# Reordering the first block pair and the last value tile of a two-branch mixing kernel

## The chip, the cores and the metric

One core of one Trainium2 chip runs the kernel. The metric is the device time of one execution in microseconds (us); lower is better. The profile shows one more execution, taken by the hardware profiler, with five engines: PE (matrix multiply; PEld is its weight load), DVE (vector), ACT (scalar and activation), POOL (GpSimd), and SP, which here issues DMAs.

## What is computed

A linear-attention branch and an expert-lookup branch on the same input `x` (2048 rows of 512) are mixed by a sigmoid gate. All data is float32. Cut to what matters:

```python
# attention: 32 heads of 16
q, k, v = split(x @ wqkv)
pq, pk = q @ w_phi[h], k @ w_phi[h]
phi_q = concat(softmax(pq), softmax(-pq)); phi_k = concat(softmax(pk), softmax(-pk))
kv = einsum("sf,sd->fd", phi_k, v);  z = sum_s phi_k
a  = ((phi_q @ kv) / (phi_q @ z + 1e-6)) @ wo
# experts: 32 heads, 16 x 16 experts, best one of each half
s1, s2 = (x @ w_q)[..., :128] @ k1.T, (x @ w_q)[..., 128:] @ k2.T
e = argmax(s1) * 16 + argmax(s2)
b = sum_h gelu(x . u[e_h]) * v[e_h]
out = g * a + (1 - g) * b,   g = sigmoid(sum(x * gate_w))
```

## The kernel before

The 2048 rows are 16 tiles of 128. float32 products are made of three matmuls of a high part and a low part: the high part is a cast (`x_high`, on ACT for tiles 3 and up), the low part the rest, by a subtraction (`x_low`, on DVE).

Every instruction stands in the program by hand: each engine works through its own queue in the order in which the lines issue, and an instruction that waits holds up all that is behind it on its engine. SP's queue of DMA issues is one of these.

**The key stage** sums phi_k and v over all 16 tiles into one PSUM bank, `kvacc`. Tiles 0 to 4 are handled one by one in the loop `for t in range(5)` (lines 416 to 448). For a tile: `vproj` and `kproj` (twelve matmuls each) make v and pk; `k_diffs` (four DVE operations) writes the softmax exponents; `k_exp` (ACT, line 266) takes the exponential; `k_sum` (DVE, lines 270 and 271) the sums and their reciprocals; `k_mult` (POOL, line 275) scales; `kvacc(t)` (PE, line 282) adds the tile to the bank. Tiles 0 to 2 have their v before the loop. In between, `score` turns two 1 MB slices of w_q at a time into score weights: four matmuls per slice (`score_w`, line 298), a copy into 16-bit planes (`wpl`, line 303), a transposing DMA (`wtp<-wpl`, line 305) and, later, `join_all`: a copy `wtj` (line 314), a cast into `sh` (line 320) and a subtraction on POOL into `sl` (line 321). A slice's buffer is free for the next load when its matmuls are done, so the loads of w_q follow `score_w`.

**The block pairs** (`for t in range(5, NT - 1, 2)`, lines 465 to 539) do tiles 5 and 6, 7 and 8, and so on, with seven products of six matmuls instead of eight (a Strassen-like scheme). `Sums.add` (POOL, lines 175 to 178) forms sums of two x tiles in place; `Sums.high` (ACT, line 183) and `Sums.low` (POOL, line 188) split them; the weights are summed once. The four weight sums are t1 (lines 388, 390 and 442), t2 (389, 441 and 446), `eh`/`el`, and the fourth, t4: a POOL subtraction `t4r` (line 448), a cast `t4h` into a free part of `sh` (line 487, ACT) and a POOL subtraction `t4l` (line 496). Only the last product of a pair uses t4:

```python
a = pks[t] = mm_bank(f"pk{t}")            # first half of pk(t)
prod(a, tile_of(t, 0), b11, True)
act.copy(b, a)                            # "pu" copy, line 483
prod(e, sums(0, 2), b1, True)
prod(b, sums(1, 0), b2, False)
act.copy(c, b)                            # "pv" copy, line 502
prod(a, tile_of(t, 2), b21, False)        # pk(t) complete
...                                       # score, kvacc
prod(b, sums(0, 0), b3, False)
act.copy(d, b)                            # "pk" copy, line 522
prod(c, sums(1, 2), b22, False)
prod(o2, tile_of(n, 2), b4, False)        # the t4 product
```

**The query loop** (lines 910 to 985) has 15 steps. In step a, queries of tile a are made (`front_q`) and their softmax run (`soft_in`, `soft_exp`, line 638, `soft_w`, `soft_b`), scores of tile a+1 are made (`front_s`), tile a-1 is transposed and joined (`planes`, `join`, line 721) and tile a-2 is multiplied by the sums (`mid_num`, line 730, with casts at line 734) and by wo (`back`, lines 839 and 846). Step 1 also ends the key stage: `vproj(15)` runs on PE, its copy `v15()` (ACT, line 254) follows, then `kvacc(15)`, then `kv_final` (ACT, line 869) copies the bank into `kvb`, which step 2's `mid_num(0)` reads. The weights of wo are cast (`wbh`, lines 942 and 978) and subtracted (`wbl`, lines 964 and 982) in the same step.

Of the kernel before, what the change touches and what calls it, by code (L numbers as in the profile page):

```python
# [16 lines left out]
ALU = mybir.AluOpType  # L17
# [18 lines left out]
def mix_kernel(ctx, tc, xT, wqT, wkT, wv, wphi, wo, wq, kk, ug, ev, cst, out):  # L36
    nc = tc.nc
    pe, dve, act, pool, sp = nc.tensor, nc.vector, nc.scalar, nc.gpsimd, nc.sync
# [112 lines left out]
    def x_high(t, ks=slice(0, NK)):  # L151
        (dve.tensor_copy if t < 3 else act.copy)(x_of(t)[0][:, ks], rawx[t][:, ks])  # L152
# [10 lines left out]
    t1r, t2r = t12[:, 0:2], t12[:, 2:4]  # L163
# [101 lines left out]
    def k_exp(t):  # L265
        act.activation(phis[t], phis[t], AF.Exp)  # L266

    def k_sum(t):
        d, st = phis[t], stk[t]
        dve.tensor_reduce(st[:, 64:128], g64(d), axis=AX.X, op=ALU.add)  # L270
        dve.reciprocal(st[:, 128:192], st[:, 64:128])
# [5 lines left out]
    def kvacc(t):  # L277
        n = F + 1 if t < NT - 1 else F
        for g in range(8):
            for c in range(4):  # L280
                h = 4 * g + c
                pe.matmul(acc[32 * c:32 * c + 32, g, :n], phis[t][:, 32 * h:32 * h + 32],
                          vs[t][:, h, :n], start=(t == 0 and g == 0),
                          stop=(t == NT - 1), skip_group_check=True)
# [131 lines left out]
    for t in range(5):  # L416
        if t in (1, 2):
            x_load(t + 6)
        if t > 2:
            vproj(t)()  # L420
        kproj(t)
        k_diffs(t)
        if t in (2, 4):
            join_all()
        score((2, 0, 1, 1, 2)[t])
        if t % 2 == 0:
            for u in (t - 3, t - 2):
                if u >= 0:
                    kvacc(u)
        if t < 3:  # L430
            x_split(t + 3)
        if t == 2:
            x_split(6)
            Sums.add(5)
        if t == 3:
            Sums.high(5)
            Sums.low(5)
        k_exp(t)
        k_sum(t)
        if t == 0:  # L440
            act.copy(t2h, t2r)
            pool.tensor_tensor(t1l, t1r, t1h, op=ALU.subtract)
        if t < 4:
            k_mult(t)
        if t == 0:
            pool.tensor_tensor(t2l, t2r, t2h, op=ALU.subtract)
        if t == 3:
            pool.tensor_tensor(t4r, t4r, t2r, op=ALU.subtract)
    x_high(7)
    x_high(8)  # L450

    def prod(o, left, right, first):
        for i, ((ah, al), (bh, bl)) in enumerate(zip(left, right)):
# [11 lines left out]
    for t in range(5, NT - 1, 2):  # L465
        n = t + 1
        more = [u for u in (t + 4, t + 5) if u < NT]
        for u in more:
            x_load(u)
        if t == NT - 5:  # L470
            rawu = [spare(ug[:, 0:2], "rawu0", [P, 2, NU])]
        elif t == NT - 3:
            rawu.append(spare(ug[:, 2:4], "rawu1", [P, 2, NU]))
            rawe = [spare(ev[:, 0], "rawe0", [P, D])]
        for u in (t + 2, t + 3):
            if u < NT - 1:
                x_low(u)
        if behind:
            k_diffs(behind)
        a = pks[t] = mm_bank(f"pk{t}")  # L480
        prod(a, tile_of(t, 0), b11, True)
        b = mm_bank(f"pu{t}")
        act.copy(b, a)
        if t + 3 < NT:
            Sums.add(t + 2)
        if t == 5:
            act.copy(t4h, by4(t4r))
        if t < NT - 3:
            join_all()
        else:  # L490
            (j6, tp), = joins
            joins.clear()
            tj6 = wa_.tile([P, D], F32, tag="wtj", bufs=1, name="wtj6")
            join_tp(j6, tp, tj6)
        if t == 5:
            pool.tensor_tensor(t4l, by4(t4r), t4h, op=ALU.subtract)
            k_mult(4)
        e = tr_bank(f"pe{t}")
        prod(e, sums(0, 2), b1, True)
        prod(b, sums(1, 0), b2, False)  # L500
        c = mm_bank(f"pv{t}")
        act.copy(c, b)
        prod(a, tile_of(t, 2), b21, False)
        k_diffs(t)
        if behind:
            k_exp(behind)
            k_sum(behind)
            k_mult(behind)
        score(1)
        if t == NT - 3:  # L510
            rawq = stage(wqT, "rawq")
        score(1)
        for u in (t - 3, t - 2):
            if u > 2:
                kvacc(u)
        k_exp(t)
        k_sum(t)
        vn, vt = v_tile(n), v_tile(t)
        act.copy(vn, by16(e))  # L519
        prod(b, sums(0, 0), b3, False)  # L520
        d = pks[n] = mm_bank(f"pk{n}")
        act.copy(d, b)
        prod(c, sums(1, 2), b22, False)
        if t == NT - 3:
            x_split(NT - 1)
        dve.tensor_tensor(vt, by16(c), vn, op=ALU.add)
        dve.tensor_tensor(vn, by16(b), vn, op=ALU.add)
        o2 = d.rearrange("p (c n) -> p c n", c=2)
        prod(o2, tile_of(n, 2), b4, False)
        if t + 3 < NT:  # L530
            Sums.high(t + 2)
            Sums.low(t + 2)
        if t == 7:
            for i in range(2):
                x_parts(i, 11)
        for u in more if n < NT - 4 else ():
            x_high(u)
        k_mult(t)
        behind = n
# [68 lines left out]
    def gelu_act(t):  # L608
        x2, gs = st8[t]["x2"], st8[t]["g"]
        act.activation(gs[:, 3:4], gs[:, 2:3], AF.Copy, scale=-0.5, bias=0.5)  # L610
        act.activation(x2, x2, AF.Tanh)
        act.activation(x2, x2, AF.Identity, bias=gs[:, 3:4], scale=gs[:, 3:4])

    def gelu_out(t):
        px, x2 = st8[t]["G"], st8[t]["x2"]
        pool.tensor_tensor(px, x2, px, op=ALU.mult)
# [18 lines left out]
    def soft_exp(t):  # L635
        d = st8[t]["ph"]
        for i in range(2):
            act.activation(hs(d, i), hs(d, i), AF.Exp)  # L638
# [77 lines left out]
    def join(t):  # L716
        e = st8[t]
        pt = w4.tile([P, 8, P], F32, tag="pt", bufs=1, name=f"pt{t}")
        p16 = pt.rearrange("p g n -> p (g n)").bitcast(U16).rearrange("p (g n j) -> p j g n", j=2, n=P)
        for i in range(2):  # L720
            act.copy(p16[:, :, 4 * i:4 * i + 4, :], e["tp"][i].rearrange("p (j g) n -> p j g n", j=2))  # L721
        e["pt"] = pt
# [187 lines left out]
    for a in range(NT - 1):  # L910
        n, b, z = a + 1, a - 1, a - 2
        owed = min(18, 3 * max(0, a - DEFER))
        left = min(18, 3 * max(0, a - DEFER + 1))
        B, Z = b >= 0, z >= 0
        if Z:
            mid_num(z)
        if B:
            planes(b, 0)
            if Z:
                c_join(z)  # L920
            planes(b, 1)
            front_q(a)
        if owed:
            back(z - 1, owed)
            store(z - 1)
        if a == 1:
            v15 = vproj(NT - 1)
        gelu_in(a)
        if Z:
            num_lo(z)  # L930
        if B:
            soft_in(a, dealt(a, b, z))
            drain(b)
        else:
            for _ in gate(a):
                pass
        gelu_act(a)
        soft_exp(a)
        if a == 1:
            v15()  # L940
            for k in range(2):
                act.copy(wbh[:, k, :], rawo[k])
        if Z and not left:
            back(z)
            store(z)
        if not left:
            mid_mask(a)
        front_s(n, 0)
        if left:
            mid_mask(a)  # L950
            if left < 18:
                back(z, 18 - left)
        if a == 1:
            kvacc(NT - 1)
            cl_.close()
            w4 = ctx.enter_context(tc_pool("w4", "right"))
        front_s(n, 1)
        front_p(n, False)
        soft_w(a)
        soft_sum(a, 0)  # L960
        soft_sum(a, 1)
        if a == 1:
            for k in range(2):
                pool.tensor_tensor(wbl[:, k, :], rawo[k], wbh[:, k, :], op=ALU.subtract)
            wo_load((2, 3))
        best(n, 0)
        soft_y(a, 0)
        soft_y(a, 1)
        soft_p(a)
        if B:  # L970
            join(b)
            gelu_out(b)
            coef(b)
            c_planes(b)
        if a == 1:
            kv_final()
            for k in range(2, NK):
                act.copy(wbh[:, k, :], rawo[k])
        soft_b(a)
        if a == 1:  # L980
            for k in range(2, NK):
                pool.tensor_tensor(wbl[:, k, :], rawo[k], wbh[:, k, :], op=ALU.subtract)
        best(n, 1)
        turn_eq(n)
        gelu_pre(n)
# [124 lines left out]
```

## Time and profile before

| | |
|---|---|
| median of 3 runs | 382.86 us (382.3 to 383.41) |
| the profiled execution | 383.04 us, of which its span is 381.3 us |
| granted TensorE clock | 1.00 |
| PE busy | 367.1 us (96% of the span) |
| DVE busy | 330.0 us (87%) |
| ACT busy | 253.0 us (66%) |
| POOL busy | 204.0 us (53%) |
| DMA | 46.67 MB, mean 122 GB/s |

Times in the rows are us from the start of the span. A timeline row gives start, duration, engine, line, operation, output<-inputs, shape and count; in brackets stands the engine's idle time before it and what ended that.

### The profile page before, as it was taken

How to read it: one execution, taken by the hardware profiler on the slowest of the kernel's cores; microseconds unless marked ns; L12 is line 12 of the kernel's file. 1: busy time of each engine (PE TensorE's matmuls, PEld its weight loads, DVE VectorE, ACT ScalarE, POOL GpSimd, SP SyncE). 2: the span in 40 equal slices, each digit the busy share in tenths (PEclk: the TensorE clock that was granted, in tenths of full speed). 3: DMA queues.
4: the chain of work that ended last, by engine and by line, in shares of the span. 5: the costliest groups of instructions: out<-in, count | busy, mean ns of one | idle time of the engine just before them, and what ended most of it. 6: DMA issues, size and time to landing. Idle time of an engine off the chain costs nothing.

```text
span 381.3 us, 8988 instructions
## 1 busy us (share of the span) xinstructions
PE 367.1 (96%) x3519; PEld 287.5 (75%) x3519; DVE 330.0 (87%) x782; ACT 253.0 (66%) x449; POOL 204.0 (53%) x206
## 2 busy tenths in 40 slices
PE   7997979999999999799999999999999999999996
PEld 3765656677778888578888888888888888888775
DVE  4679888899968858979999999999999999999993
ACT  4584677757666344678677686695686686686741
POOL 1175889898938733756335344364364364364700
PEclk9999999999999999999999999999999999999999
DMA  7865697599664034141541452434513523613211
GB/s 265 314 247 162 224 301 250 180 189 286 236 181 71 4 84 81 58 98 42 110 98 44 83 99 65 89 82 44 126 43 84 124 44 83 126 43 83 60 39 55
DMA packets 72218, 46.67 MB, mean 122 GB/s; under 512 B 63600, under 2 KB 64496, under 8 KB 69872
## 3 DMA queue, kind: packets, MB, share of 16 engines
q1 hardware_dynamic: 71312, 45.24, 44.7%
q10 hardware_dynamic: 864, 0.87, 0.8%
q8 instruction: 27, 0.44, 0.5%
q14 instruction: 15, 0.12, 0.1%
HBM read 26.43 MB, written 4.19 MB: 80 GB/s over the span
## 4 chain that ended last, share of the span: by engine, by line
PE 76%; POOL 7%; DVE 5%; ACT 4%; DMA 4%; issue 3%; ACTq 0%; POOLq 0%
PE po L839 11%; PE s L56 7%; PE s L57 7%; PE s L58 7%; PE po L846 5%; PE pq L56 5%; PE pq L58 4%; PE pq L57 4%; PE pk L455 3%; PE oT L730 3%; DMA wtp<-wpl 2%; PE pp L57 2%; PE pp L58 2%; PE pp L56 2%; PE pu L455 2%
## 5 line engine op out<-in xcount | busy, mean ns | idle before, releaser
L644 POOL TENSOR_TENSOR w<-d,zb 128x512 f32<-128x512 f32 x32 | 40.9, 1296 | 83.4 <-ACT d L638 83.4
L56 PE MATMUL s<-sh,xh 128*128 128x512 f32 x128 | 51.0, 399 | 0.0
L57 PE MATMUL s<-sl,xh 128*128 128x512 f32 x128 | 49.9, 390 | 0.0
L58 PE MATMUL s<-sh,xl 128*128 128x512 f32 x128 | 49.9, 390 | 0.0
L638 ACT ACTIVATE d<-d 128x512 f32<-128x512 f32 x32 | 20.1, 632 | 39.9 <-DVE d L119 31.1
L679 POOL TENSOR_TENSOR d<-d,st 128x512 f32<-128x512 f32 x30 | 31.2, 1062 | 28.4 <-DVE st L673 25.5
L275 POOL TENSOR_TENSOR d<-d,st 128x1024 f32<-128x1024 f32 x16 | 32.5, 2030 | 17.7 <-ACT v L519 7.8
L721 ACT COPY pt<-tp 128x1024 uint16<-128x1024 uint16 x28 | 36.4, 1370 | 0.0
L711 ACT COPY pl<-d 128x1024 uint16<-128x1024 uint16 x28 | 29.2, 1045 | 4.3 <-POOL d L679 4.3
L58 PEld LDWEIGHTS s<-sh,xl 128*128 128x128 f32 x128 | 24.0, 188 | 5.1
L56 PEld LDWEIGHTS s<-sh,xh 128*128 128x128 f32 x128 | 24.0, 188 | 4.7
L57 PEld LDWEIGHTS s<-sl,xh 128*128 128x128 f32 x128 | 24.1, 188 | 4.5
L56 PE MATMUL pq<-wah,xh 128*128 128x512 f32 x64 | 26.8, 418 | 0.0
L648 DVE TENSOR_REDUCE st<-d 128x32 f32<-128x512 f32 x32 | 21.7, 682 | 5.4 <-ACT d L638 3.8
L58 PE MATMUL pq<-wah,xl 128*128 128x512 f32 x64 | 25.1, 392 | 0.0
L57 PE MATMUL pq<-wal,xh 128*128 128x512 f32 x64 | 25.0, 390 | 0.0
L270 DVE TENSOR_REDUCE st<-d 128x64 f32<-128x1024 f32 x16 | 19.3, 1204 | 5.9 <-ACT d L266 5.8
L839 PE MATMUL po<-wbh,xh 128*128 128x512 f32 x60 | 24.0, 400 | 0.0
L266 ACT ACTIVATE d<-d 128x1024 f32<-128x1024 f32 x16 | 17.0, 1061 | 9.8 <-DVE d L121 9.6
L839 PE MATMUL po<-wbl,xh 128*128 128x512 f32 x60 | 23.4, 391 | 0.0
L688 DVE TENSOR_TENSOR eq<-s,mx 128x512 bf16<-128x512 f32 x32 | 22.1, 691 | 1.2
L156 DVE TENSOR_TENSOR xl<-xr,xh 128x512 fp32r<-128x512 f32 (+2 forms) x17 | 21.1, 1261 | 2.0 <-ACT xh L152 1.9
(240 smaller groups left out, 1104.2 us busy)
## 6 DMA issues: line engine op xcount, KB each, us to landing
wq<-wq SPq DMA_DIRECT2D x16, 1024.0 KB, 5.2
xr<-xT SPq DMA_DIRECT2D x15, 256.0 KB, 5.3
y<-ot SPq DMA_DIRECT2D x15, 256.0 KB, 2.4
rawk<-wkT SPq DMA_DIRECT2D x1, 1024.0 KB, 6.5
rawq<-wqT SPq DMA_DIRECT2D x1, 1024.0 KB, 6.3
rawo<-wo SPq DMA_DIRECT2D x4, 256.0 KB, 3.6
rawu<-ug SPq DMA_DIRECT2D x2, 258.0 KB, 3.4
rawv<-wv ACTq DMA_DIRECT2D x2, 256.0 KB, 4.9
```

What stands on the lines that cost most here:

```text
L56: pe.matmul(o, ah, bh, start=(first and i == 0), stop=False)
L57: pe.matmul(o, ah, bl, start=False, stop=False)
L58: pe.matmul(o, al, bh, start=False, stop=(last and i == n - 1))
L156: dve.tensor_tensor(l[:, ks], rawx[t][:, ks], h[:, ks], op=ALU.subtract)
L275: pool.tensor_tensor(g64(d), g64(d), b64(st[:, 128:192]), op=ALU.mult)
L644: pool.tensor_tensor(hs(e["w"], i), hs(e["ph"], i), hs(zb, i), op=ALU.mult)
L648: dve.tensor_reduce(pair(e["st"][:, 64:128])[:, :, i], hs(e["ph"], i), axis=AX.X, op=ALU.add)
L679: eng.tensor_tensor(g64(d)[:, gs_], g64(d)[:, gs_], r[:, gs_].unsqueeze(2).to_broadcast([P, 32, F]), op=ALU.mult)
L688: dve.tensor_tensor(e["eq"][:, 512 * half:512 * half + 512].rearrange("p (h f) -> p h f", f=F), p3, mx.unsqueeze(2).to_broadcast([P, H, F] ...
L711: act.copy(pl, e["ph"][:, halves[i]].bitcast(U16).rearrange("p (c j) -> p j c", j=2))
L721: act.copy(p16[:, :, 4 * i:4 * i + 4, :], e["tp"][i].rearrange("p (j g) n -> p j g n", j=2))
L839: pe.matmul(po, a, b, start=(i == 0), stop=False)
```

## The change

Four things are placed elsewhere; no operation is added or removed.

- The fourth weight sum: `t4r` goes from the end of tile 3 to tile 0, behind `t1l`; its cast `t4h` from block pair 5 to tile 0; `t4l` from block pair 5 to behind `t2l` at tile 0.
- `kvacc(0)` goes from tile 2 to tile 3.
- `x_high(7)` and `x_high(8)` go from the end of the loop to tile 3, ahead of `Sums.high(5)`; `k_exp(4)` and `k_sum(4)` go from tile 4 into block pair 5, behind the pu copy and `Sums.add(7)`. On DVE, `k_sum(4)` so comes behind `x_low(7)` and `x_low(8)`.
- In step 1 of the query loop, `v15()` goes ahead of `soft_exp(1)`, and `kv_final` goes from behind `c_planes(0)` to ahead of `gelu_out(0)`, right behind `join(0)`.

```diff
@@ for t in range(5) @@
         score((2, 0, 1, 1, 2)[t])
-        if t % 2 == 0:
-            for u in (t - 3, t - 2):
-                if u >= 0:
-                    kvacc(u)
+        for u in ((), (), (), (0,), (1, 2))[t]:
+            kvacc(u)
         if t < 3:
             x_split(t + 3)
         if t == 2:
             x_split(6)
             Sums.add(5)
         if t == 3:
+            x_high(7)
+            x_high(8)
             Sums.high(5)
             Sums.low(5)
-        k_exp(t)
-        k_sum(t)
+        if t < 4:
+            k_exp(t)
+            k_sum(t)
         if t == 0:
             act.copy(t2h, t2r)
             pool.tensor_tensor(t1l, t1r, t1h, op=ALU.subtract)
+            pool.tensor_tensor(t4r, t4r, t2r, op=ALU.subtract)
+            act.copy(t4h, by4(t4r))
         if t < 4:
             k_mult(t)
         if t == 0:
             pool.tensor_tensor(t2l, t2r, t2h, op=ALU.subtract)
-        if t == 3:
-            pool.tensor_tensor(t4r, t4r, t2r, op=ALU.subtract)
-    x_high(7)
-    x_high(8)
+            pool.tensor_tensor(t4l, by4(t4r), t4h, op=ALU.subtract)
@@ block pairs @@
             Sums.add(t + 2)
         if t == 5:
-            act.copy(t4h, by4(t4r))
+            k_exp(4)
+            k_sum(4)
...
         if t == 5:
-            pool.tensor_tensor(t4l, by4(t4r), t4h, op=ALU.subtract)
             k_mult(4)
@@ query loop @@
         gelu_act(a)
+        if a == 1:
+            v15()
         soft_exp(a)
         if a == 1:
-            v15()
             for k in range(2):
                 act.copy(wbh[:, k, :], rawo[k])
...
             join(b)
+            if a == 1:
+                kv_final()
             gelu_out(b)
             coef(b)
             c_planes(b)
         if a == 1:
-            kv_final()
             for k in range(2, NK):
                 act.copy(wbh[:, k, :], rawo[k])
```

## The prediction

> **What bounds the kernel now.** I read the page first, then busy time by stage, then PE's timeline with its idle times, and last the queues of POOL, ACT and DVE around each idle time.
>
> ```profile
> PE 367.1 (96%) x3519; PEld 287.5 (75%) x3519; DVE 330.0 (87%) x782; ACT 253.0 (66%) x449; POOL 204.0 (53%) x206
> ```
>
> ```profile
> 166.00:366.00 200.00, 200.00 (x1451) 163.62 (x1450) 189.53 (x546) 145.80 (x274) 93.87 (x98) 1.00 0.37 78
> ```
>
> Page, then the stage from 166 to 366 (PE, PEld, DVE, ACT, POOL). PE is never without work in those 200 us, at full granted clock; an order can only bring what PE idles elsewhere. DVE has 10.5 us free there, in 13.5 steps of the loop: 0.8 a step. PE's timeline shows six waits over 0.3 us between 30 and 165, all but one ahead of lines that the change touches:
>
> ```profile
> 32.48 0.74 PE L282 MATMUL kvacc<-v,d 128*32 128x17 f32 x64 [1.91 <-POOL d L275]
> ...
> 47.25 1.29 PE L282 MATMUL kvacc<-v,d 128*32 128x17 f32 x128
> ...
> 53.49 0.50 PE L455 MATMUL pu<-uh,xh 128*128 128x512 f32 x1 [1.99 <-ACT pu L483]
> ...
> 58.97 0.50 PE L455 MATMUL pu<-eh,gh 128*128 128x512 f32 x1
> ...
> 62.84 0.50 PE L455 MATMUL pk<-sl,xh 128*128 128x512 f32 x1 [0.51 <-POOL sl L496]
> ...
> 64.09 0.39 PE L455 MATMUL pk<-wah,xh 128*128 128x512 f32 x1
> ...
> 66.43 0.50 PE L455 MATMUL pe<-t1h,gl 128*128 128x512 f32 x1 [0.36 <-POOL gl L188]
> ...
> 156.08 0.74 PE L282 MATMUL kvacc<-v,d 128*32 128x16 f32 x64 [1.99 <-ACT v L254]
> ...
> 162.09 1.21 PE L730 MATMUL oT<-pt,kvb 64*32 64x128 f32 x32 [0.83 <-ACT kvb L869]
> ...
> 166.08 0.39 PE L839 MATMUL po<-wbh,xh 128*128 128x512 f32 x1
> ...
> 170.16 0.36 PE L749 MATMUL mk<-wm,et 128*128 128x16 bf16 x8
> ```
>
> The waits add up to 1.91 + 1.99 + 0.51 + 0.36 = 4.77 in the front and 1.99 + 0.83 = 2.82 in step 1, 7.6 us in all. That is the ceiling. What is kept of it depends on what comes late next, part by part.
>
> **Part 1a, kvacc(0) at tile 3.** PE no longer waits at 30.6 for k_mult(0), and runs 1.9 us ahead. kvacc(0)'s own 0.7 us are only moved. The next thing that PE needs from POOL is k_mult(2), for the second half of the row at 47.25: reached at 47.25 + 0.65 = 47.9 before, now at 46.0. When is k_mult(2) done? POOL's queue, with the t4 subtractions in its holes:
>
> ```profile
> 30.50 1.93 POOL L275 TENSOR_TENSOR d<-d,st 128x1024 f32<-128x1024 f32 x1 [2.41 <-DVE st L271]
> 32.39 2.40 POOL L446 TENSOR_TENSOR ul<-xraw,uh 128x1024 fp32r<-128x1024 f32 x1
> 37.20 1.94 POOL L275 TENSOR_TENSOR d<-d,st 128x1024 f32<-128x1024 f32 x1 [2.41 <-DVE st L271]
> ...
> 41.61 0.74 POOL L175 TENSOR_TENSOR xr<-xr 128x256 f32<-128x256 f32 x1 [1.23 <-DVE xl L156]
> ...
> 44.76 1.94 POOL L275 TENSOR_TENSOR d<-d,st 128x1024 f32<-128x1024 f32 x1
> ...
> 77.17 1.29 POOL L188 TENSOR_TENSOR gl<-xr,gh 128x512 fp32r<-128x512 f32 x1
> 78.42 1.75 POOL L188 TENSOR_TENSOR xl<-xr,xh 128x512 fp32r<-128x512 f32 x1
> ```
>
> ```profile
> 10.07 0.69 DVE L156 TENSOR_TENSOR xl<-xr,xh 128x512 fp32r<-128x512 f32 x1
> ...
> 32.59 2.75 DVE L156 TENSOR_TENSOR xl<-xr,xh 128x512 fp32r<-128x512 f32 x1
> ...
> 53.69 2.25 DVE L156 TENSOR_TENSOR xl<-xr,xh 128x512 fp32r<-128x512 f32 x2
> ...
> 56.61 0.69 DVE L115 TENSOR_REDUCE st<-pk 128x32 f32<-128x512 f32 x1 [0.68 <-PE pk L455]
> ...
> 78.15 2.57 DVE L156 TENSOR_TENSOR xl<-xr,xh 128x512 fp32r<-128x512 f32 x2
> ```
>
> The two holes of 2.41 are as long as t4r and t4l, subtractions of the shape that takes 2.40 at 32.39, so the bare price is nothing. But x_low on DVE takes 0.69 at 10.07 with POOL idle and 2.75 at 32.59, where it ends 0.55 after POOL's subtraction (32.39 + 2.40): it stands still while POOL subtracts. Between two POOL operations back to back it gets a turn: at 78.15 the pair takes 2.57, and the POOL operation that follows the first 1.75 instead of 1.29, so a turn costs POOL 0.45. The Trainium skill ("SBUF — State Buffer", Who interferes with whom) says that a DVE instruction with two SBUF inputs contends with a GpSimd instruction that reads SBUF, and that the one that issues first blocks the other fully. The trace agrees on the blocking, 2.75 against 0.69; on who wins at a hand-over only the 1.75 speaks.
>
> New POOL times, from 30.50 - 2.41 = 28.1: t4r with a DVE turn 2.85, to 30.9; k_mult(0) 1.9, to 32.8; t2l with a turn 2.85, to 35.6; t4l 2.4, to 38.0. So k_mult(1) starts at 38.0 instead of 37.20, 0.8 late. The hole of 1.23 ahead of Sums.add(5) takes that up, but DVE's turns put 0.45 or 0.9 back: k_mult(2) starts at 45.1 (between 44.76 and 45.4) and ends at 47.0. PE waits 1.0 at kvacc(2). **Kept of the 1.91: 0.8.** DVE itself gains: x_low(4) takes its turn at 32.8 and no longer ends at 35.34; the wait for later POOL work gives most of that back.
>
> On ACT the cast t4h waits for t4r until 30.9, with x_high(4) and k_exp(1) queued behind it:
>
> ```profile
> 32.71 1.06 ACT L266 ACTIVATE d<-d 128x1024 f32<-128x1024 f32 x1 [4.43 <-DVE d L121]
> ...
> 52.86 0.57 ACT L483 COPY pu<-pk 128x512 f32<-128x512 f32 x1
> ...
> 56.41 1.37 ACT L314 COPY wtj<-wtp 128x1024 uint16<-128x1024 uint16 x1 [1.85 <-DMA wtp<-wpl]
> ```
>
> The hole there is 4.43 long; t4h (1.06, like the exp of the same shape) and x_high(4) (half of that) end at 32.5, just ahead of k_exp(1) at 32.71. Price nothing; without that cover, up to 0.5 on ACT.
>
> **Part 1b, the pu copy.** PE had finished the pe product at 51.50 and waited until the copy at 52.86 was done. Ahead of that copy ACT had k_exp(4), held by DVE, and two x_high. Both now stand elsewhere: x_high in ACT's waits for Sums.add(5) at tile 3, k_exp(4) behind the copy. The copy then follows the wpl copy at once. That chain hangs on Sums.high(5), so on POOL's Sums.add(5), and is 0.3 late with it: done at 50.8. PE arrives at 51.50 - 0.8 = 50.7. **Kept: 1.9 of 1.99.** PE is 2.7 ahead.
>
> **Part 1c, the rest of block pair 5.** b is overwritten at 58.97 only after the pv copy has read it, and that copy stands on ACT behind wtj at 56.41, which waits for a transposing DMA. So this row, which shows no wait, had no slack: pv copy done at 58.92 by 56.41 plus the 2.5 of wtj, cast and copy. PE now comes at 56.3. The DMA is issued right after the wpl copy, at 50.0 as before, so all hangs on its time to land. SP's queue, then the landings of the transposes issued at 41.88 and at 50.01:
>
> ```profile
> 35.79 4.51 SPq L143 DMA_DIRECT2D wq<-wq  x2
> 41.88 1.24 SPq L305 DMA_TRANSPOSE wtp<-wpl  x1
> 46.64 1.19 SPq L143 DMA_DIRECT2D wq<-wq  x2
> 50.01 1.24 SPq L305 DMA_TRANSPOSE wtp<-wpl  x1
> ```
>
> ```profile
> DMA to landing us min/median/max: 4.0/4.0/4.0
> ```
>
> ```profile
> DMA to landing us min/median/max: 6.3/6.3/6.3
> ```
>
> The first had one load of w_q under way, issued by 40.3; the second had two, issued by 47.8. These two go when score_w has freed their buffers, and PE does that 1.9 us sooner now, while the transpose is not sooner. I take 4.0, the row that is nearest to loads further on their way. Then wtj starts at 54.1, pv is done at 56.6, and PE waits 0.3. At 6.3 PE would wait 2.6.
>
> The next gate is the pk copy, behind k_exp(5) and k_diffs(5). k_diffs(5) started at 56.61, held by PE. Now PE is ready at 53.9, and DVE comes last: x_low(8), which ended at 53.69 + 2.25 = 55.94, ends some 2.2 sooner, as t4r no longer stands ahead of the POOL operations that it waits for, and k_sum(4), now behind it, takes some 1.7 for a reduction and a reciprocal (an estimate; the reduction is twice as long as the 0.69 at 56.61, for twice the elements), so k_diffs(5) starts at 55.4. The pk copy moves by about as much, with 0.7 more as wtj no longer holds ACT: PE starts the last product some 1.9 sooner, at 59.9. The 0.51 for t4l is gone, as t4l is done at 38.0. **Block pair 7 starts at 61.4 instead of 64.09: 2.7.** There the 0.36 goes too: POOL has 2.4 less ahead of that gl, and its operations moved by more than PE. **Part 1: 2.7 + 0.36 = 3.1**, between 0.9 (the DMA lands late) and 4.8 (all waits gone). Pairs 7 to 13 show one wait of 0.17, so the lead stays.
>
> **Part 2, step 1.** v15's copy is the only thing that PE waited for at 156.08, and it stood behind exponentials that wait for DVE. Ahead of them it has nothing to wait for but its own matmuls, and only ACT's idle time behind it. The 1.99 goes.
>
> ```profile
> 160.99 0.62 ACT L798 COPY plc<-cf 128x512 uint16<-128x512 uint16 x1 [1.42 <-POOL cf L793]
> 161.52 1.07 ACT L869 COPY kvb<-kvacc 32x128 f32<-32x128 f32 x4
> ...
> 165.08 0.63 ACT L734 CAST xh<-oT 128x256 fp32r<-128x256 f32 x2
> ```
>
> ```profile
> L882 SPq DMA_DIRECT2D rawo<-wo x1: 328/328/328, 159.5 to 159.5; - x1
> ...
> DMA to landing us min/median/max: 3.1/3.1/3.1
> ```
>
> ```profile
> 168.76 0.42 DVE L830 TENSOR_TENSOR cl<-ctj,ch 128x256 fp32r<-128x256 f32 x1
> ```
>
> kv_final, four copies, 1.07, fits the 1.42 in which ACT waited for POOL: ACT is free at 160.99 - 1.42 = 159.6, or 159.1 without v15's copy, and kvb is done at 160.1 instead of 161.52 + 1.07 = 162.6, so PE's oT ends 2.4 sooner. But then ACT stands where it stood: the plc copy waits for POOL until 161.0 as before, and of the two wo casts the second waits for its load, issued at 159.5 and landed 3.1 later, at 162.6. So casts and gelu copies run until 164.45, and the oT cast starts there instead of at 165.08. `back(0)` needs its first half: PE starts it at 164.8 instead of 166.08 and waits 1.2 for it. Then cl, which DVE has 0.55 sooner (168.76 + 0.42 - 0.55 = 168.6), is needed at 168.5, as the last two of 18 matmuls in 4.1. `back(0)` ends at 169.05 instead of 170.16. **Part 2: 1.1** of 2.82; bounds 0.6 (cast alone) and 2.4 (kvb alone). DVE's 0.8 free per step lets it follow PE after that.
>
> **The sum.** The profiled execution took 383.04 us, span 381.3: 383.04 - 3.1 - 1.1 = 378.84. It lies 0.18 over the median of 382.86, so **378.7 us**, a span of 377.1.
>
> **The rivals.** 0.3%, 1.15 us, is about what a measurement of this kernel can tell from no change.
> - *The transposing DMA still lands 6.3 after its issue.* pv is done at 58.9 as before, and of 2.7 only the 0.51 and 0.36 remain: 382.86 - 0.9 - 1.1 = 380.9. For it: landings of this kind differ by 2.3 for the same bytes. Against: its loads start earlier. 0.13.
> - *Step 1 gives nothing*, as wo load, POOL and DVE hold back(0) where it was; 382.86 - 3.1 = 379.8. For it: cl at 168.76 is followed closely by its use. 0.09.
> - *The change does not do what it says*: the waits wander to kvacc(2) and the pv copy and come back whole, 382.5. 0.06.
> - *Slower: POOL back to back starves DVE.* If x_low gets no turn at a hand-over, x_low(3) waits through t4r and x_low(4) through t2l and t4l, 2.4 each, and the key stage's DVE chain runs 4.8 late, less the hole of 1.23: 3.6 late at k_mult(2), pu and pv copy. With part 2, 382.86 + 3.6 - 1.1 = 385.4. It decides once DVE loses more than 1.1 + 1.15 = 2.3 in that chain. For it: the 2.75. Against: the 1.75, a turn given. 0.06. By the sentence of the Trainium skill named above, if the next POOL operation counts as issued first, this is the outcome.
>
> **The numbers.** The forecast has 0.66. Faster: 0.66 + 0.13 + 0.09 = 0.88; within 0.3% 0.06; slower 0.06. The range goes from 377.5 (part 2 at its upper bound) to 381.2 (just past the late DMA).
>
> **What would show it.** In the changed profile: no wait at kvacc near 30, but one of about 1 us for k_mult(2) near 46; x_low(4) ending near 33.3; pu without a wait over 0.2; the third landing of wtp near 4.0; no wait on sl of t4; pair 7 starting near 61.4; in step 1 no wait for v, kvb copied 1 us ahead of plc, and a new wait of about 1.2 ahead of `back(0)`, by the oT cast. Wrong would make it: a long wait at the pv copy, x_low over 3 us at tiles 3 or 4, or new waits in pairs 7 to 13.

## The result, and the profile after

| | median us | runs | against the kernel before on the same chip |
|---|---|---|---|
| before | 383.41 (382.3 to 384.19) | 5 | |
| changed | 379.4 (378.71 to 380.43) | 5 | ratio 0.9904 [0.9876, 0.9933] |

The changed kernel is 4.0 us faster by its median (2.6 to 4.8 by the interval of the ratio); 378.7 was forecast. The span of the profiled execution is only 2.7 shorter, 378.6 for 381.3: its last output copy comes 4.0 sooner, but 1.3 more pass from there to its end. First the page of the changed kernel (its busy times) and the stage that was full before, columns as there:

```profile
PE 366.6 (97%) x3519; PEld 287.7 (76%) x3519; DVE 330.4 (87%) x782; ACT 253.2 (67%) x449; POOL 205.8 (54%) x206
```

```profile
166.00:366.00 200.00, 200.00 (x1484) 163.39 (x1483) 189.70 (x550) 143.80 (x271) 92.73 (x96) 1.00 0.36 78
```

Nothing changed there: PE has the same work and is still never idle in those 200 us, so what was gained ahead of them is kept. Next, PE's timeline of the changed kernel: all its waits over 0.17 us from 30 to 166 but one (0.28 at 132.86, for zc, which the kernel before has too), with five rows that mark where PE stands. The stretch between the two rows of line 749 is what I call step 1 here; `back(0)` is its last part.

```profile
29.70 1.06 PE L298 MATMUL ws<-wq,kp 128*32 128x512 f32 x8
...
47.32 0.74 PE L282 MATMUL kvacc<-v,d 128*32 128x17 f32 x64 [1.22 <-POOL d L275]
...
57.02 0.50 PE L455 MATMUL pu<-eh,gh 128*128 128x512 f32 x1 [0.74 <-ACT pv L502]
...
61.62 0.39 PE L455 MATMUL pk<-wah,xh 128*128 128x512 f32 x1
...
63.44 0.39 PE L455 MATMUL pe<-t1h,gl 128*128 128x512 f32 x1
...
147.42 0.36 PE L749 MATMUL mk<-wm,et 128*128 128x16 bf16 x8
...
156.05 1.22 PE L730 MATMUL oT<-pt,kvb 64*32 64x128 f32 x32 [0.35 <-ACT kvb L869]
...
161.36 0.50 PE L839 MATMUL po<-wbh,xh 128*128 128x512 f32 x1 [1.14 <-ACT xh L734]
...
165.56 0.73 PE L846 MATMUL po<-eh,cl 128*128 128x512 f32 x2 [0.20 <-DVE cl L830]
...
166.14 0.36 PE L749 MATMUL mk<-wm,et 128*128 128x16 bf16 x8
```

Two of these marks in the kernel before, which the prediction did not show:

```profile
29.51 1.07 PE L298 MATMUL ws<-wq,kp 128*32 128x512 f32 x8
...
150.91 0.36 PE L749 MATMUL mk<-wm,et 128*128 128x16 bf16 x8
```

Subtracting gives the lead at each place. At 29.70 PE is 0.19 late, by the first loads and so not by the change; I add this to each lead and call the sum net. Block pair 7 starts 64.09 - 61.62 = 2.47 earlier (net 2.66), step 1 begins 150.91 - 147.42 = 3.49 earlier (net 3.68) and ends 170.16 - 166.14 = 4.02 earlier (net 4.21). From there to the last output copy the lead stays at 4.0. Six long waits are gone or small; five shorter ones stand in their places. These leads are of one execution: in a2 and a3 below, the same kernel, the net lead is 3.64 and 3.03 before step 1 and 4.03 and 3.55 behind it.

How the front came about, in the queues of POOL, DVE and ACT of the changed kernel, and the landing of the third transposing DMA (KB, then us to landing; it has no KB):

```profile
28.23 2.84 POOL L444 TENSOR_TENSOR xraw<-xraw,xraw 128x1024 f32<-128x1024 f32 x1
31.03 1.94 POOL L275 TENSOR_TENSOR d<-d,st 128x1024 f32<-128x1024 f32 x1
32.94 2.87 POOL L449 TENSOR_TENSOR ul<-xraw,uh 128x1024 fp32r<-128x1024 f32 x1
35.75 2.40 POOL L450 TENSOR_TENSOR sl<-xraw,sh 128x1024 fp32r<-128x1024 f32 x1
38.09 2.45 POOL L275 TENSOR_TENSOR d<-d,st 128x1024 f32<-128x1024 f32 x1
...
45.33 1.93 POOL L275 TENSOR_TENSOR d<-d,st 128x1024 f32<-128x1024 f32 x1
```

```profile
32.79 0.73 DVE L156 TENSOR_TENSOR xl<-xr,xh 128x512 fp32r<-128x512 f32 x1
```

```profile
31.11 1.05 ACT L445 CAST sh<-xraw 128x1024 fp32r<-128x1024 f32 x1 [3.14 <-POOL xraw L444]
...
50.19 0.59 ACT L483 COPY pu<-pk 128x512 f32<-128x512 f32 x1
...
54.45 1.38 ACT L314 COPY wtj<-wtp 128x1024 uint16<-128x1024 uint16 x1 [2.20 <-DMA wtp<-wpl]
```

```profile
wtp<-wpl SPq DMA_TRANSPOSE x1, 4.1
```

POOL now works without a hole from 28.2 to 40.5. The operations that follow a waiting DVE subtraction are 0.44 to 0.51 longer than their bare 2.40 and 1.94: that is DVE's turn, and x_low(4) takes it at 32.79 and is done at 33.5.

Step 1 of the changed kernel on ACT, POOL (line 606 is a product for the gelu) and DVE, and the row of line 767 in the kernel before:

```profile
155.49 1.06 ACT L869 COPY kvb<-kvacc 32x128 f32<-32x128 f32 x4
157.49 0.62 ACT L798 COPY plc<-cf 128x512 uint16<-128x512 uint16 x1 [0.94 <-POOL cf L793]
...
159.01 0.62 ACT L980 CAST wbh<-rawo 128x512 fp32r<-128x512 f32 x1 [0.38 <-DMA rawo<-wo]
...
160.96 0.63 ACT L734 CAST xh<-oT 128x256 fp32r<-128x256 f32 x2
```

```profile
160.34 2.52 POOL L984 TENSOR_TENSOR wbl<-rawo,wbh 128x512 fp32r<-128x512 f32 x2
162.83 0.73 POOL L606 TENSOR_TENSOR x<-x,px 128x256 f32<-128x256 f32 x1
```

```profile
162.87 0.73 DVE L767 TENSOR_TENSOR m<-sa 128x32 uint16<-128x32 uint16 x1
...
165.09 0.42 DVE L830 TENSOR_TENSOR cl<-ctj,ch 128x256 fp32r<-128x256 f32 x1
```

```profile
167.11 0.17 DVE L767 TENSOR_TENSOR m<-sa 128x32 uint16<-128x32 uint16 x1
```

kvb is copied ahead of plc, as the change has it, but `back(0)` still hangs on the second wo load, the oT cast behind it, and cl.

### The profile page after: what moved, and what is told of

It is laid out like the page before. It is cut to its first block, busy times and chain, and to the rows that moved or that the text cites. A ratio compares the mean times of both kernels' runs of the same rounds, so it can differ in the third digit from the quotient of the medians.

```text
span 378.6 us, 8986 instructions
## 1 busy us (share of the span) xinstructions
PE 366.6 (97%) x3519; PEld 287.7 (76%) x3519; DVE 330.4 (87%) x782; ACT 253.2 (67%) x449; POOL 205.8 (54%) x206
## 4 chain that ended last, share of the span: by engine, by line
PE 85%; DVE 4%; POOL 4%; DMA 4%; ACT 2%; issue 1%; SPq 0%; POOLq 0%; ACTq 0%; DVEq 0%
PE po L839 10%; PE s L56 8%; PE s L57 7%; PE s L58 7%; PE po L846 5%; PE pk L455 5%; PE pq L56 4%; PE pq L58 4%; PE pq L57 4%; PE pu L455 3%; PE ws L298 3%; PE oT L730 2%; PE pp L57 2%; PE pp L58 2%; PE pp L56 2%; PE kvacc L282 2%
## 5 line engine op out<-in xcount | busy, mean ns | idle before, releaser
L275 POOL TENSOR_TENSOR d<-d,st 128x1024 f32<-128x1024 f32 x16 | 33.4, 2089 | 13.1 <-ACT v L519 7.1
L687 DVE TENSOR_REDUCE mx<-s 128x32 f32<-128x512 f32 x32 | 21.8, 681 | 0.0
```

The source lines that it names most:

```text
L275: pool.tensor_tensor(g64(d), g64(d), b64(st[:, 128:192]), op=ALU.mult)
L687: dve.tensor_reduce(mx, p3, axis=AX.X, op=ALU.max)
```

## The experiments

The edits are against the changed kernel. Medians in us; each ratio is to the kernel before on the same chip.

| run | us | ratio |
|---|---|---|
| e1_front_only | 379.72 | 0.989 [0.9864, 0.9916] |
| e2_step1_only | 383.76 | 0.9997 [0.9975, 1.0019] |
| e3_kvacc0_back | 382.69 | 0.997 [0.995, 0.9989] |
| e4_t4_late | 382.56 | 0.9962 [0.9944, 0.998] |
| e5_pu_behind | 382.63 | 0.9949 [0.992, 0.9978] |
| e6_kvacc2_late | 379.07 | 0.9877 [0.9827, 0.9927] |
| e7_wbl_by_memset | 380.02 | one run |
| a2_changed_again | 379.17 | 0.9864 [0.9829, 0.9898] |
| a3_changed_third | 379.52 | 0.9889 [0.986, 0.9919] |
| e8_pv_first | 379.09 | 0.987 [0.9841, 0.99] |
| e9_wo_behind | 379.85 | 0.9889 [0.9856, 0.9921] |
| e10_all_three | 378.85 | 0.9871 [0.984, 0.9903] |

**The two parts apart.** e1 puts `v15()` and `kv_final` back where they were; e2 undoes all the rest, that is the first three points of the change.

```diff
e1, step 1
-        if a == 1:
-            v15()
         soft_exp(a)
         if a == 1:
+            v15()
...
-            if a == 1:
-                kv_final()
...
         if a == 1:
+            kv_final()
```

> The changed kernel without its edit of step 1: v15's copy stands behind the exponentials of step 1 again and kv_final behind the plc copy. Theory (the two parts are independent, and the front alone gave the lead of 3.48 us with which PE enters step 1): 3.5 us faster than before, the two waits of 1.99 and 0.83 back in step 1. Rival (the parts overlap: the front's lead is partly eaten in step 1 by DVE and POOL, and the edit of step 1 is what keeps it): under 3.0 us faster, with waits in step 1 that are longer than before.

> The kernel before with the edit of step 1 alone. Theory (the edit's 2.82 us of waits turn into a wait of 1.1 for the oT cast and 0.2 for cl, because DVE meets POOL's second wo subtraction and loses 0.55): 0.5 us faster than before, L767 on DVE at 0.7 instead of 0.17. Rival (the prediction's sum, where DVE is 0.55 sooner): 1.1 us faster, L767 at 0.17.

In e1 PE enters step 1 with a net lead of 3.67, as in the changed kernel, and leaves it with 3.65; in e2 it gains 0.51 there (from 0.37 behind to 0.14 ahead). The parts add up: 3.67 + 0.51 = 4.18 of 4.21. So step 1 is worth 0.5 by the profiles, not 1.1. The times say less: the interval of e2 allows anything from a loss of 0.7 to a gain of 1.0. The wait for v came back in e1, the 0.83 for kvb did not, as PE ran at half clock ahead of it. The wait, and the stretch behind it (PEclk is the third column from the end):

```profile
152.08 0.95 PE L282 MATMUL kvacc<-v,d 128*32 128x16 f32 x64 [1.98 <-ACT v L254]
```

```profile
152.30:155.70 3.40, 3.40 (x68) 2.79 (x56) 3.37 (x7) 3.36 (x4) 3.40 (x4) 0.50 0.10 33
```

**Why step 1 gave less.** e7 replaces the last two subtractions into wbl by writes of zero.

```diff
-                pool.tensor_tensor(wbl[:, k, :], rawo[k], wbh[:, k, :], op=ALU.subtract)
+                pool.memset(wbl[:, k, :].bitcast(F32), 0.0)
```

> The changed kernel with POOL's two last wo subtractions replaced by memsets of zero: the low parts of two of the four slices of wo are left out. Theory (DVE's L767, with both inputs in SBUF, stood still in step 2 while POOL read SBUF for the second subtraction): L767 takes 0.17 instead of 0.73, cl comes 0.5 sooner and PE's wait of 0.20 for it is gone; PE leaves back(0) 0.2 to 0.3 sooner. Rival (L767 was long for another reason, or a POOL write holds it as well): L767 near 0.7 again, the wait for cl stays.

DVE's rows of e7:

```profile
163.92 0.20 DVE L765 TENSOR_TENSOR m<-sa 128x64 uint16<-128x64 uint16 x1
164.04 0.17 DVE L767 TENSOR_TENSOR m<-sa 128x32 uint16<-128x32 uint16 x1
```

Line 767 takes 0.17 again, and no wait for cl is left. But it was not the subtraction itself that had held it. In the changed kernel the subtractions are over at 162.86, and line 767, from 162.87 to 163.60, runs beside POOL's line 606, from 162.83 to 163.56. That product had all its inputs at 161.05 and stood behind the two subtractions. In e7 the memsets are over at 162.22 and line 606 at 163.10, before DVE is there at 163.92. (Counted from the row that starts step 1, line 606 comes 1.4 sooner in e7 and DVE 0.3 later, so it would have missed DVE without that delay too.) Which DVE operation is hit depends on when it comes: in a2, the same kernel as changed, line 765 takes 0.70 instead of 0.20 beside line 606, and line 767 takes 0.16. So POOL's subtractions do it by pushing line 606 onto DVE's short operations.

The cost lies in `back(0)`. From its first matmul to the next row of line 749 it takes 4.78 in the changed kernel and 4.25 in e7; 4.25 is also what the prediction has (169.05 - 164.8). The bracket of 0.20 before the last two matmuls shows less than half of that 0.53: it counts from the end of the matmul before, while the row starts 0.60 behind that one, where the beat is 0.23, and takes 0.58 to the next row, for 0.45 in the kernel before. Step 1 gains 0.74 in e7 and not 1.1, because the second wo load and with it the oT cast came later there (ACT waits 0.69 for the load instead of 0.38).

The Trainium skill ("SBUF — State Buffer", Who interferes with whom) says that a two-input DVE instruction contends with a GpSimd instruction that reads SBUF and not with one that only writes it. The first half agrees with 0.73 for 0.17 beside line 606; the second no run here shows.

**The parts of the front.** e3 only puts kvacc(0) back to tile 2. e4 puts t4r, t4h and t4l back to where they were. e5 puts x_high(7), x_high(8), k_exp(4) and k_sum(4) back ahead of the pu copy.

```diff
e3, key stage
-        for u in ((), (), (), (0,), (1, 2))[t]:
+        for u in ((), (), (0,), (), (1, 2))[t]:
e4: the same four lines, taken out of tile 0
+        if t == 3:
+            pool.tensor_tensor(t4r, t4r, t2r, op=ALU.subtract)
... block pair 5
             k_sum(4)
+            act.copy(t4h, by4(t4r))
...
         if t == 5:
+            pool.tensor_tensor(t4l, by4(t4r), t4h, op=ALU.subtract)
             k_mult(4)
e5
-            x_high(7)
-            x_high(8)
...
-        if t < 4:
-            k_exp(t)
-            k_sum(t)
+        k_exp(t)
+        k_sum(t)
... behind the loop
+    x_high(7)
+    x_high(8)
... block pair 5
-        if t == 5:
-            k_exp(4)
-            k_sum(4)
```

> The changed kernel with kvacc(0) at tile 2 again. Theory (kvacc(0)'s place sets when the two w_q loads of tile 4 start, and they set when the transposing DMA of pair 5 lands): PE waits 2.4 at kvacc near 31 for k_mult(0), which ends at 33.0; no wait for k_mult(2); the loads go out 2 us later, the third landing of wtp is near 6 instead of 4.1, and PE waits over 1.5 at the pv copy; 2 us slower than the changed kernel, so 2 us faster than before. Rival (the landing does not depend on the loads): landing near 4.1, no wait at pv, 1 us slower than the changed kernel or less.

> The changed kernel with the fourth weight sum in its old places: t4r at the end of tile 3, t4h and t4l in pair 5. Theory (POOL's order there is the next bound): k_mult(2) ends some 0.5 sooner, so the wait at kvacc(2) is 0.7 instead of 1.22, but t4l ends near 62 while PE wants it at 60, and POOL's gl of pair 7 is late too: waits of 2 and 0.5 there; 2 to 2.5 us slower than the changed kernel. Rival (POOL has slack, and the holes merely hold what would fit anyway): within 0.5 us of the changed kernel.

> The changed kernel with x_high(7), x_high(8) and k_exp(4), k_sum(4) in their old places, ahead of the pu copy. Theory (what stands ahead of the pu copy on ACT sets when PE may start its product): the pu copy starts at 53.2 and PE waits 3 us for it, from 50.7; the transposing DMA lands as in the changed kernel, so its wait of 0.74 at the pv copy is covered; 1.7 to 2 us slower than the changed kernel, 2 us faster than before. Rival (the gate of the pair is the pv copy or the pk copy, not the pu copy): within 0.5 us of the changed kernel.

Against the kernel before on the same chip, e3, e4 and e5 keep 1.2, 1.5 and 2.0 us by their ratios, where the changed kernel has 3.7 (5.2 and 4.3 in a2 and a3). So each edit costs some 2 to 3 us; 2 were expected for e3 and e5. By the profiles it costs more than its own wait. e3 keeps a net lead of only 0.6 of 4.2: PE's rows and the third landing of e3:

```profile
32.99 0.74 PE L282 MATMUL kvacc<-v,d 128*32 128x17 f32 x64 [2.25 <-POOL d L275]
...
59.50 0.50 PE L455 MATMUL pu<-eh,gh 128*128 128x512 f32 x1 [1.82 <-ACT pv L502]
...
89.61 0.50 PE L455 MATMUL pk<-sh,xh 128*128 128x512 f32 x1 [0.79 <-ACT pk L522]
```

```profile
wtp<-wpl SPq DMA_TRANSPOSE x1, 6.6
```

With kvacc(0) early, `score_w` is late and frees its buffers late, the two loads of w_q are issued at 47.1 instead of 44.7, the transposing DMA stands close behind them and lands in 6.6 instead of 4.1. That is the rival of the late DMA, brought back by one line. The 0.79 at 89.61 is another matter: it follows a landing of 10.4 of the fifth transposing DMA, issued 2.3 behind its loads. e7 and e9, whose front is that of the changed kernel, have 0.79 and 0.40 at the same place with landings of 10.2 and 9.8, issued at the same distance; in the changed kernel it is 7.7. So this wait comes and goes without an edit, and it is part of what e3, e4 (0.51) and e5 (0.77) lose.

In e4 the wait for t4l at the t4 product, which I expected, did not appear, since PE was held earlier. The pv copy stands on ACT behind wtj, which starts 1.3 later than in the changed kernel. The cast t4h ahead of it has waited for t4r and ends at 55.13, and POOL's line 321, also behind t4r, releases it at 55.73. But the third transposing DMA landed in 5.5 here, at 55.6, so the DMA alone would have held wtj nearly as long. e4 on ACT, then on PE, then the stretch that follows:

```profile
54.08 1.05 ACT L488 CAST sh<-xraw 128x1024 fp32r<-128x1024 f32 x1 [2.06 <-POOL xraw L449]
55.76 1.35 ACT L314 COPY wtj<-wtp 128x1024 uint16<-128x1024 uint16 x1 [0.64 <-POOL sl L321]
```

```profile
58.30 0.50 PE L454 MATMUL pu<-eh,gh 128*128 128x512 f32 x1 [1.94 <-ACT pv L503]
```

```profile
59.20:62.50 3.30, 3.30 (x10) 2.52 (x9) 1.77 (x2) 2.49 (x4) 3.30 (x3) 0.50 1.37 325
```

The last column but two, the granted clock, is 0.50. A net lead of 0.9 is left, so this execution loses 3.3, the late landing and the half-clock stretch included, where 2 to 2.5 were expected. In e5 the pu wait is back in full, and again half clock follows; nothing of the lead is left (0.6 behind, net):

```profile
53.25 0.50 PE L454 MATMUL pu<-uh,xh 128*128 128x512 f32 x1 [2.78 <-ACT pu L482]
```

```profile
54.70:58.00 3.30, 3.30 (x11) 1.90 (x14) 0.30 (x1) 1.89 (x3) 3.01 (x5) 0.50 0.09 34
```

So the three edits of the front need each other: each of them, taken away alone, takes over half of the whole gain with it. How much of that is the half clock in e4 and e5, and how much the late landings, is not separated here.

**The wait that is left at kvacc(2).** e6 moves kvacc(2) into block pair 5.

```diff
-        for u in ((), (), (), (0,), (1, 2))[t]:
+        for u in ((), (), (), (0,), (1,))[t]:
... block pairs
-            if u > 2:
+            if u > 1:
                 kvacc(u)
```

> The changed kernel with kvacc(2) in pair 5, beside kvacc(3), so that PE does not wait 1.22 for k_mult(2) at tile 4. Theory (ACT and the transposing DMA set the pair, and PE only waits elsewhere): a wait of about 0.9 at the pu copy and one of about 0.7 or more at the pv copy, pair 7 starts as in the changed kernel; within 0.3 us of it. Rival (the wait at kvacc(2) is what PE loses): 1.2 us faster than the changed kernel.

```profile
48.37 0.50 PE L455 MATMUL pe<-t1h,gl 128*128 128x512 f32 x1 [0.51 <-POOL gl L188]
...
50.55 0.50 PE L455 MATMUL pu<-uh,xh 128*128 128x512 f32 x1 [0.98 <-ACT pu L483]
...
59.87 0.50 PE L455 MATMUL pk<-sh,xh 128*128 128x512 f32 x1 [0.31 <-ACT pk L522]
```

The 1.22 and the 0.74 at the pv copy are gone, and 0.51, 0.98 and 0.31 stand in their places. Pair 7 starts with a net lead of 2.65, against 2.66: no gain.

**Attempts to go on from there**, with the changed kernel twice more beside them.

> The changed kernel once more, for the comparison on this chip: 4.0 us faster than before; waits and leads as in its first profile, to 0.1 us from the third weight load on. Open is the granted clock: in two of the four kernels run so far PE ran 3.41 us at half clock right after a wait of almost 2 us. Theory (a wait of 2 us can fall so that a half-clock stretch follows; 1.2 us does not do it): no such stretch between 10 and 370 us here, while runs of before show one or two of them in most executions, by mean clocks of 0.991 to 0.996. Rival (it comes at random): half-clock stretches here as in the others.

> The changed kernel, unchanged, beside the three attempts on the same chip: 379.2 to 379.4 us by the two lists so far.

a2 has no half-clock stretch ahead of its last output copy. Its waits at pv and for the oT cast are 0.15 and 0.28 longer than in the first profile, so they repeat less well than the 0.1 expected.

> The changed kernel, with two moves in pair 5 alone: the pv copy is placed ahead of the joining of the third turned plane, so it no longer stands behind the wait for that transposing DMA (2.20 us idle on ScalarE before line 314 in the changed kernel), and the pk copy (line 522) is placed ahead of tile 5's exponential. Theory: the wait of 0.74 us at pu<-eh,gh goes, nothing takes its place before pair 7, and PE is 0.5 to 0.7 us earlier from there to the end: about 378.8 us where the changed kernel gives 379.4. Rival: pair 7's first sums or its wq loads are next, then the 0.74 us come back as waits in pair 7 and the time stays at 379.4.

```diff
e8, pair 5: join_all() and k_exp(5) move
         act.copy(c, b)
+        if t == 5:
+            join_all()
...
         act.copy(d, b)
+        if t == 5:
+            k_exp(t)
+            k_sum(t)
+            act.copy(vn, by16(e))
```

The pv wait goes and pair 7 starts 1.2 net ahead of the changed kernel's. Then this falls to 0.2, at this place of e8 (PE, then the exponential ahead of the pk copy on ACT):

```profile
71.94 0.50 PE L455 MATMUL pk<-sh,xh 128*128 128x512 f32 x1 [0.90 <-ACT pk L527]
```

```profile
67.48 1.06 ACT L266 ACTIVATE d<-d 128x1024 f32<-128x1024 f32 x1 [1.38 <-DVE d L121]
```

The rival holds for the larger part, by pair 7's low parts: two x_low operations on DVE take 3.49 beside POOL's work, from 61.56, the exponential waits for DVE behind them, and the pk copy stands behind that. The transposing DMA is not the gate here: its plane landed 1.9 sooner than in the changed kernel, and ACT still waits 1.38 for DVE after it.

> The changed kernel, with the casts of the third and fourth slices of wo on ScalarE and their subtractions on POOL placed behind the casts of oT in step 2, and the two products with those low parts placed last among the oT products of that step. Theory: the wait of 1.14 us for the cast of oT falls to under 0.3 us, and the end of the step is then set by cl on VectorE (ends at 165.51 in the changed kernel, 0.5 to 0.8 us earlier here): 0.4 to 0.8 us faster than the changed kernel, about 378.8 us. Rival: the subtractions on POOL end later and stand before cl, and the wait only moves from oT to cl: no gain, 379.4 us.

```diff
e9: taken out of step 1, and in step 2
             mid_num(z)
+        if a == 2:
+            for k in range(2, NK):
+                act.copy(wbh[:, k, :], rawo[k])
+            for k in range(2, NK):
+                pool.tensor_tensor(wbl[:, k, :], rawo[k], wbh[:, k, :], op=ALU.subtract)
... back_mm
+        if t == 0:
+            mms = mms[:5] + mms[6:7] + mms[8:] + [mms[5], mms[7]]
```

DVE and PE of e9:

```profile
162.29 1.29 DVE L767 TENSOR_TENSOR m<-sa 128x32 uint16<-128x32 uint16 x1
```

```profile
163.60 0.50 PE L841 MATMUL po<-wbl,xh 128*128 128x512 f32 x1 [0.48 <-POOL wbl L923]
...
166.02 0.73 PE L848 MATMUL po<-eh,cl 128*128 128x512 f32 x2 [0.99 <-DVE cl L830]
```

In e9 the oT wait is gone, and 0.48 and 0.99 came in its place: POOL's subtractions now lie fully on DVE's operations ahead of cl, and line 767 takes 1.29. The rival holds; step 1 gives 0.39, against 0.53 in the changed kernel and 0.39 in a2.

> The two kernels e8 and e9 together, with tile 2's key-value sums moved to pair 5 and the cast behind the second turned plane placed behind the pu copy. Theory: the gains add, and of the 1.22 us before tile 2's sums 0.3 to 0.7 us are saved too: 1.2 to 2.0 us faster than the changed kernel, about 377.8 us. Rival: as in the run that only moved tile 2's sums, the wait turns up again at pair 5's low half and its pu copy: then about 378.4 us, by the sum of the other two alone.

Its edits are those of e8, e9 and e6, and in pair 5 `join_end` of the second turned plane behind the pu copy. e10 shows both returns, 1.00 at pk in pair 7 and 1.00 at cl; the hoped-for 1.2 to 2.0 did not come. Its median is 0.67 below that of a3, and five of its six runs lie below all six of a3. But the intervals of the ratios overlap (0.9871 [0.984, 0.9903] and 0.9889 [0.986, 0.9919]), as do those of e8 and a3, and its net lead behind step 1 is 4.07, no more than the 4.21 of the changed kernel's first profile: that a version beats the changed kernel is not shown.

## Why the prediction was right, and where not

**Part 1a held.** t4r 28.2 to 31.1 (28.1 to 30.9 foreseen), k_mult(1) from 38.1 (38.0), k_mult(2) from 45.33 (45.1), x_low(4) done at 33.5 (33.3). The wait at kvacc(2) is 1.22, and 1.0 was foreseen. DVE is given its turn: the slower rival fell here, and with it the reading that POOL's next operation would count as first.

**Part 1b held.** The pu copy is done at 50.78 (50.8), and there is no wait.

**Part 1c held, with small errors.** The landing is 4.1 (4.0), wtj starts at 54.45 (54.1), and the wait at the pv copy is 0.74 for 0.3. It is the least certain place: in a2 and a3, the same kernel, the landing is 4.2 and 5.0 and the wait 0.89 and 1.65. The reason given, loads that start earlier, is what e3 tested. Pair 7 starts at 61.62 (61.4).

**The rest of the front was sized too small.** "0.36 too" was the only gain that I counted behind pair 7's start. The lead grows there from 2.47 to 3.44 by the pu product. The bracket of 0.36 cost 0.63: its row starts 0.75 behind the one before, and the next 0.34 behind it, where 0.23 is the beat. A hole that the prediction did not count cost 0.33 in the same way, at 68.14. Front: 3.68 net, for 3.1; but 3.03 in a3, and 2.56 and 2.78 in e7 and e9, which have the same front.

**Step 1 was sized too large.** Up to the oT cast the working holds: foreseen 164.45, less the lead of 3.49 is 160.96, which is the measured start; the wait is 1.14 for 1.2. The step that failed is "cl, which DVE has 0.55 sooner": cl ends at 165.51, which is 169.18 - 165.51 - 3.49 = 0.18 sooner. Ahead of line 767 DVE was 0.75 sooner, and line 767 lost 0.56 of that. The 0.55 was carried through DVE's queue without asking what POOL does meanwhile: its line 606, pushed back by the wo subtractions, lay on that operation (e7). A wait of 0.35 for kvb, which I did not name, cost nothing behind the oT cast. Step 1: 0.53, for 1.1.

The two misses, +0.6 and -0.6, cancel: 4.21 net of the late start, for 4.2. That the total came so close is partly luck: it is 4.03 in a2 and 3.55 in a3.

**The rivals.** The late DMA did not come in the changed kernel, but e3 shows that it was one edit away. "Step 1 gives nothing" named the right hands (wo load, POOL, DVE) and was half right. Waits do wander, to kvacc(2) and pv, at 1.22 and 0.74 of 3.90 removed. New waits in pairs 7 to 13, named as a sign of being wrong, are absent in the changed kernel's three profiles, but e7 and e9 have one by a late landing. The half clock (below) is in none of the sums.

## What to carry to other kernels

When several waits of one engine lie in a row, sum what is left by following each queue to the next gate, and expect edits to need each other: undoing any one of three here took back some 2 to 3 us of 4. A wait costs more than its bracket shows, 0.63 for 0.36 here, so size it by the starts of the rows around it. Before counting an operation as sooner on DVE, look at what POOL will be doing at that moment, behind all that its queue holds. And after a change that removes waits, the place to look next is a DMA whose landing depends on how closely it stands behind a large load, since moving it forward may make it land no sooner.

## What the hardware showed that I had not expected

**Half clock after waits of some 2 us.** In e1, e4 and e5 the granted clock is 0.50 for one stretch of 3.41 us that begins within 1.4 us of the end of a PE wait of 1.98, 1.94 and 2.78. No wait of 1.82 or less was followed by one, and neither were those of 1.99 in the profiled run of before or of 2.25 in e3, so such a wait is not enough by itself. The mean clocks of whole runs fit: beside a3, 10 of 11 runs of before have 0.991 to 0.996 (one stretch makes 0.9955), and all 6 of a3 at least 0.999. The mean is a rough sign, for idle time at the end counts too: the 0.997 of the changed kernel's profile comes from there. The Trainium skill ("TensorE: Matmul & The Clock Gate", HAM oscillation) gives idle gaps above some 3.4 us as what to avoid; here gaps of 1.94 sufficed. What a stretch costs stays open: of the runs of before with 0.991, two took 382.96 and 383.01 and one 385.68. In e1 the stretch takes the place of another wait: step 1 lasts 19.27 there, without the 0.83 for kvb, and 19.25 in before. By their medians a2 and a3 are 5.3 and 4.9 faster than before, more than any sum here has; whether that is the half clock, which before has there and they have not, is open.

**The third transposing DMA lands at a time set by the loads ahead of it.** From the issue of two 1 MB loads to that of the transposing DMA, and its landing: 3.2 and 6.6 (e3), 3.4 and 6.3 (before), 4.9 and 4.7 (e10), 5.6 and 4.1 (changed). The sum stays at 9.3 to 9.9 in 12 of the 14 profiles. In a3, also 5.6 after the first load's issue, the second load was issued 1.2 later than in the changed kernel's first profile, and the landing was 5.0; in e4 the sum is 11.0, for which I have no reason. The sum is no constant of such DMAs: for the four planes that follow it goes from 8.9 to 12.8. That the loads are what the third waits for is argued from these rows; no run took them away.
